# Scores of an attention kernel in two matmuls of 288 columns, and first-pass scores of batch 0 on 128 rows

## The chip, the cores and the metric

The kernel runs on one core of one Trainium2 chip. The metric is the device time of one execution in microseconds (us), lower is better: the median of three runs of the kernel before is 1108.2 us (1106.79 to 1108.76).

## What is computed

Attention over 4 batches, 8 heads, 576 positions and a head dimension of 64, with a threshold: of each row of scores only those within tau of the row's maximum are kept. Behind it come two feed-forward layers over the 2304 tokens (512 to 2048 to 512), the first with a hard-swish gate, the second with a sigmoid gate. All in float32.

```python
scores = scale * np.matmul(q, k.transpose(0, 1, 3, 2))
thresh = np.max(scores, axis=-1, keepdims=True) - tau
scores = np.where(scores >= thresh, scores, -1000000000.0)
scores = scores - np.max(scores, axis=-1, keepdims=True)
attn = np.exp(scores)
attn = attn / (np.sum(attn, axis=-1, keepdims=True) + 1e-09)
return np.matmul(attn, v).astype(np.float32)
```

The result, heads side by side, goes through `g = h * clip(h + 3, 0, 6) / 6` between the first pair of weight matrices and through `g = h * sigmoid(1.702 h)` between the second.

## The kernel before, in words

**Units.** `unit` (line 512) handles two heads of one batch, 16 units in all, four for a batch. Its nine query tiles (line 515) are four tiles of 128 queries for each head and one remainder tile, `None`, that holds the last 64 queries of both heads. A tile's scores against all 576 keys go to a buffer `ps` of two PSUM banks, of which there are two (lines 578 and 594). `soft` (line 610) then reduces the row maximum on VectorE (line 620), makes the threshold (line 622 or 624), takes the exponential on ScalarE (line 625) and multiplies it by the mask on VectorE, summing up the row (line 626); after that the `ps` buffer is free.

**Batches 1 to 3** (units 4 to 15, function `full`). To get float32 results from the faster matmul type fp32r, q and k are split into a high and a low part (lines 555 to 562), and the high and low part of q lie on top of one another in the 128 rows. `score2` (line 576) runs k high and then k low, each as a matmul of 512 and one of 64 columns (lines 582 and 583), so four matmuls for a tile and eight for the remainder tile, which takes both heads. In batches 2 and 3 the tiles of e are turned by VectorE and by transfers through DRAM (`blocks`, line 693), in batch 1 by TensorE (`plain`, line 685).

**Batch 0** (units 0 to 3, function `half`, line 788) works in plain fp32: `score` (line 592) multiplies 64 rows of q with 64 rows of k in two matmuls of 288 columns, one head in rows 0 to 63, the other in rows 64 to 127. The first pass takes the first 256 queries of each head, four tiles for a unit, one at a time; the second pass takes the remainder tile on all 128 rows and then the other four tiles in pairs, one of each head together. The queries come in one buffer of 640 columns by four transfers (line 537) and two zero fills (line 535), the keys by two transfers (line 541); VectorE scales the queries by 1/8 (line 547). The first passes of all four units are entered ahead of the second passes, with the first MoE half of batch 0 (`moe_a`, line 836) between.

**Order.** All operations are entered in a `Plan` (line 61) with an engine, a cost in ns and a nominal time, and what they read and write. `settle` (line 220) places them by list scheduling, forward and backward in turn, on the five engines and the DMA, and the program of every engine is emitted in that order. `score2` has a planned cost of 4 or 8 times `pe(SH)`, SH being 288 (line 589). `fill` (line 233) puts matmuls of zeros and ones (line 1134) where the plan leaves TensorE idle. All transfers are issued by SP in the planned order, and each waits in that queue for its buffer. A ring such as `g` (line 807, eight buffers) hands its buffers out in turn.

Of the kernel before, what the change touches and what calls it, by code (L numbers as in the profile page):

```python
# [18 lines left out]
P = 128  # L19
# [242 lines left out]
def tile_top_attention_moe_moe2(  # L262
# [22 lines left out]
    FULL = EXACT = 4  # L285
# [226 lines left out]
    def unit(u, b, j, t0):  # L512

        early, exact = u < FULL, u < EXACT
# [8 lines left out]
        def tile_():  # L523
            return buf("kqv", 12, "st", [P, QC], F32R)

        if exact:
            khb, qhb = tile_(), tile_()
        pieces = [(0, 0, 0, S)] + ([(1, 0, 0, 256), (1, 256, 320, 256), (1, 576, 256, 64)] if b == 0 else [(1, 0, 64, 512), (1, 576, 0, 64)])

        def of_head(x, hd):  # L530
            return [(x, ("z", hd))] + [(x, (h, o)) for h, o, _, _ in pieces if h == hd]

        def load_q(x, ap):
            for hd, z in ((0, 576), (1, 512)):
                add(POOL, 100, K("ld"), "qz", lambda hd=hd, z=z: nc.gpsimd.memset(ap()[64 * hd:64 * hd + 64, z:z + 64], 0.0), [], [(x, ("z", hd))])
            for hd, o, i, n in pieces:
                move(K("ld"), "ldq", 256 * n, lambda hd=hd, o=o, i=i, n=n: nc.sync.dma_start(out=ap()[64 * hd:64 * hd + 64, o:o + n], in_=q2[b, 2 * j + hd, :64, i:i + n]), [], [(x, (hd, o))])

        def load_k(x, ap):
            for hd in range(2):  # L540
                move(K("ld"), "ldk", 256 * S, lambda hd=hd: nc.sync.dma_start(out=ap()[64 * hd:64 * hd + 64, :S], in_=k2[b, 2 * j + hd, :64]), [], [(x, hd)])

        if exact:
# [32 lines left out]
        def score2(s):  # L576

            ps, t = buf("ps", 2, "ps", [P, 1024]), tiles[s]

            def mm(hd, q0, st, sp):  # L580
                for w, a, z in ((khs, st, False), (kls, False, sp)):
                    for c0, c1 in ((0, 512), (512, S)):
                        nc.tensor.matmul(ps.t[:, c0:c1], qss[hd].t[:, q0:q0 + P], w[hd].t[:, c0:c1], start=a, stop=z)  # L583

            def run():
                for hd in range(2) if t is None else t[:1]:
                    mm(hd, t[1] * P + 128 * hd if t else 0 if hd else 512, t is not None or hd == 0, t is not None or hd == 1)

            add(PE, (4 if t else 8) * pe(SH), K("S", s), "S", run, [x[hd] for hd in (range(2) if t is None else t[:1]) for x in (qss, khs, kls)], [ps])
            soft(s, ps, lambda: ps.t[:, :S], lambda e: e.t)  # L590

        def score(ss):

            pss = {s: buf("ps", 2, "ps", [P, 1024]) for s in ss}

            def two(s, n=512):
                return pss[s].t.rearrange("p (j s) -> p j s", j=2)[:, :, :n]

            def mm():
                for i in range(2):  # L600
                    for s in ss:
                        t = tiles[s]
                        rows, q0 = (slice(0, P), 512) if t is None else (slice(64 * t[0], 64 * t[0] + 64), t[1] * P)
                        nc.tensor.matmul(two(s)[:, i, :SH], f32(qhb.t)[rows, q0:q0 + P], f32(khb.t)[rows, i * SH:(i + 1) * SH], start=True, stop=True)  # L604

            add(PE, 4 * 243 + 300 + 40 * (len(ss) > 1), K("S", ss[0]), "S", mm, [qhb, khb] if len(ss) > 1 or tiles[ss[0]] is None else of_head(qhb, tiles[ss[0]][0]) + [(khb, tiles[ss[0]][0])], [pss[s] for s in ss])
            for s in ss:
                soft(s, pss[s], lambda s=s: two(s, SH), lambda e: e.t.rearrange("p (j s) -> p j s", j=2))

        def soft(s, ps, scores, like):  # L610
# [6 lines left out]
            def ev():  # L617
                return like(e)

            add(DVE, 665, K("R", s), "R", lambda: nc.vector.tensor_reduce(out=nm.t[:, c], in_=scores(), op=ALU.max, axis=AX.XY if len(scores().shape) == 3 else AX.X, negate=True), [ps], [(nm, s)])  # L620
# [4 lines left out]
            add(ACT, 624, K("X", s), "X", lambda: nc.scalar.activation(out=ev(), in_=scores(), func=ACTF.Exp, bias=nm.t[:, c]), [ps, (nm, s)], [e])  # L625
            add(DVE, 729, K("M", s), "M", lambda: nc.vector.scalar_tensor_tensor(out=ev(), in0=scores(), scalar=th.t[:, c], in1=ev(), op0=ALU.is_ge, op1=ALU.mult, accum_out=sm.t[:, c]),  # L626
# [566 lines left out]
```

## Time and profile before

| | us |
|---|---|
| median of three runs | 1108.2 |
| lowest and highest | 1106.79, 1108.76 |
| the profiled execution | 1111.02 |
| its span, first to last instruction | 1108.9 |

The span is what the profile's shares refer to. PE is TensorE's matmuls, PEld its weight loads, DVE VectorE, ACT ScalarE, POOL GpSimd, SP the engine that issues the transfers. Times of rows in order of time count from the start of the span. The end of a matmul in the trace is modelled and runs past the start of the next, so the price of a matmul is read from one start to the next. The granted clock is TensorE's, as a share of full speed (2.4 GHz); it has two levels, 1.0 and 0.5, and a stretch shows their mean. An fp32 matmul stands in the trace as two records, an fp32r matmul as one.

### The profile page before, as it was taken

To read this page: it belongs to the slowest core of one execution; us is meant where nothing else is said; L and a number is where in the kernel's file an instruction comes from. 1 tells how busy PE (TensorE), PEld (TensorE's weight loads), DVE (VectorE), ACT (ScalarE), POOL (GpSimd) and SP (SyncE) were. 2 spreads that over 40 slices of the span, in tenths; PEclk is the share of its full clock that TensorE was granted. 3 is DMA by queue.
4 is the path that set the end of the run, shared out by engine and by line. 5 is a ranking of instruction groups with operands and counts; after the bars stand their busy time and mean duration, and the time that the engine had idled before them with its cause. 6 is when DMAs were issued, how large, how long until landed. Compare 5 with 4: busy or idle time off the path is not lost.

```text
span 1108.9 us, 20750 instructions
## 1 busy us (share of the span) xinstructions
PE 1076.6 (97%) x7672; PEld 973.6 (88%) x7672; DVE 729.0 (66%) x1482; ACT 639.3 (58%) x1340; POOL 510.2 (46%) x590
## 2 busy tenths in 40 slices
PE   8999999999899999999999999999999999999998
PEld 6677788977788889899999999989998889889888
DVE  6788866667687776267877432778787674653634
ACT  4698767665575655466555323566656665443533
POOL 1578867765686755356466223551313322001100
PEclk8899999998999999999999999999999999999999
DMA  6234322256878686635664312335545443312202
GB/s 201 91 116 132 101 82 59 91 147 191 221 234 247 182 253 186 182 107 157 203 204 128 91 54 65 124 103 169 180 145 175 151 136 115 114 39 77 91 1 72
DMA packets 89733, 150.19 MB, mean 135 GB/s; under 512 B 8864, under 2 KB 50976, under 8 KB 87584
## 3 DMA queue, kind: packets, MB, share of 16 engines
q1 hardware_dynamic: 89632, 148.87, 44.1%
q8 instruction: 60, 0.98, 0.4%
q14 instruction: 41, 0.34, 0.1%
HBM read 101.52 MB, written 47.32 MB: 134 GB/s over the span
## 4 chain that ended last, share of the span: by engine, by line
PE 77%; DVE 8%; DMA 7%; ACT 4%; issue 2%; POOL 2%; SPq 0%; DVEq 0%; POOLq 0%; ACTq 0%
PE py L834 24%; PE pm L814 16%; PE pm L971 13%; PE pm L834 7%; PE ps L583 5%; PE pm L755 5%; PE pm L677 3%; PE ps L604 2%; DMA qk<-in_k_dram 1%; DVE e L626 1%; DVE nm L620 1%; DVE outlring L369 1%; PE pm L736 1%; DVE tc L369 1%; ACT e L625 1%
## 5 line engine op out<-in xcount | busy, mean ns | idle before, releaser
L834 PE MATMUL py<-g,outhring 128*128 128x512 f32 (+2 forms) x1152 | 288.1, 337 | 2.0 <-DVE g L369 1.4
L834 PEld LDWEIGHTS py<-g,outhring 128*128 128x128 f32 x1152 | 193.7, 188 | 20.7 <-DVE g L369 4.0
L834 PE MATMUL py<-g,outlring 128*128 128x512 f32 (+2 forms) x576 | 193.4, 336 | 0.0
L814 PE MATMUL pm<-xh,inhring 128*128 128x256 f32 (+1 forms) x512 | 155.6, 304 | 0.2
L814 PE MATMUL pm<-xl,inhring 128*128 128x256 f32 (+1 forms) x512 | 150.8, 295 | 0.0
L814 PE MATMUL pm<-xh,inlring 128*128 128x256 f32 (+1 forms) x512 | 150.8, 294 | 0.0
L971 PE MATMUL pm<-outhring,inhring 128*128 128x256 f32 x512 | 144.5, 282 | 3.4 <-ACT u L366 1.9
L971 PE MATMUL pm<-outlring,inhring 128*128 128x256 f32 x512 | 143.7, 281 | 0.0
L971 PE MATMUL pm<-outhring,inlring 128*128 128x256 f32 x512 | 143.5, 280 | 0.0
L620 DVE TENSOR_REDUCE nm<-ps 128x1 f32<-128x576 f32 x144 | 106.5, 751 | 44.5 <-PE ps L583 37.5
L626 DVE SCALAR_TENSOR_TENSOR e<-ps,th,e 128x576 f32<-128x576 f32 x128 | 102.6, 811 | 35.6 <-ACT e L625 34.8
L369 POOL TENSOR_TENSOR g<-t,g 128x256 fp32r<-128x256 f32 (+1 forms) x104 | 87.2, 842 | 82.1 <-ACT g L366 76.3
L826 DVE SCALAR_TENSOR_TENSOR t<-t,pm 128x256 f32<-128x256 f32 (+1 forms) x128 | 57.1, 448 | 95.3 <-ACT t L825 94.9
L834 PEld LDWEIGHTS py<-g,outlring 128*128 128x128 f32 x576 | 108.2, 188 | 10.0
L834 PE MATMUL pm<-g,outhring 128*128 128x256 f32 (+1 forms) x512 | 109.9, 307 | 0.0
L369 POOL TENSOR_TENSOR wmstg<-wmstg,wrstg 128x512 uint32<-128x512 uint32 x48 | 64.6, 1346 | 94.9 <-DVE wmstg L422 75.3
L369 POOL TENSOR_TENSOR g<-tc,g 128x512 fp32r<-128x512 f32 x24 | 31.9, 1328 | 165.1 <-ACT g L366 160.3
L825 ACT ACTIVATE t<-pm,half 128x256 f32<-128x256 f32 (+1 forms) x128 | 63.5, 498 | 72.7 <-PE pm L814 66.5
L971 PEld LDWEIGHTS pm<-outhring,inhring 128*128 128x128 f32 x512 | 96.8, 189 | 7.3 <-ACT u L366 2.3
L583 PE MATMUL ps<-kqv 128*128 128x512 f32 x480 | 93.6, 326 | 9.3 <-DVE e L626 9.1
L625 ACT ACTIVATE e<-ps,nm 128x576 f32<-128x576 f32 x128 | 93.1, 733 | 16.5 <-DVE nm L620 14.8
L971 PEld LDWEIGHTS pm<-outlring,inhring 128*128 128x128 f32 x512 | 96.9, 189 | 2.5
(110 smaller groups left out, 2452.0 us busy)
## 6 DMA issues: line engine op xcount, KB each, us to landing
turned<-tr SPq DMA_DIRECT2D x16, 1024.0 KB, 4.6
et<-turned SPq DMA_DIRECT2D x64, 256.0 KB, 5.9
wrawstg<-in_w1i_dram SPq DMA_DIRECT2D x16, 512.0 KB, 3.8
wrawstg<-in_w1o_dram SPq DMA_DIRECT2D x16, 512.0 KB, 3.7
wrawstg<-in_w2i_dram SPq DMA_DIRECT2D x16, 512.0 KB, 3.7
wrawstg<-in_w2o_dram SPq DMA_DIRECT2D x16, 512.0 KB, 4.0
qk<-in_k_dram SPq DMA_DIRECT2D x24, 288.0 KB, 4.2
qk<-in_q_dram SPq DMA_DIRECT2D x24, 288.0 KB, 4.2
```

Of the source, the lines that this page charges most:

```text
L369: return lambda: (nc.vector if eng == DVE else nc.gpsimd).tensor_tensor(out=o(), in0=a(), in1=b(), op=op)
L583: nc.tensor.matmul(ps.t[:, c0:c1], qss[hd].t[:, q0:q0 + P], w[hd].t[:, c0:c1], start=a, stop=z)
L620: add(DVE, 665, K("R", s), "R", lambda: nc.vector.tensor_reduce(out=nm.t[:, c], in_=scores(), op=ALU.max, axis=AX.XY if len(scores().shape ...
L625: add(ACT, 624, K("X", s), "X", lambda: nc.scalar.activation(out=ev(), in_=scores(), func=ACTF.Exp, bias=nm.t[:, c]), [ps, (nm, s)], [e])
L626: add(DVE, 729, K("M", s), "M", lambda: nc.vector.scalar_tensor_tensor(out=ev(), in0=scores(), scalar=th.t[:, c], in1=ev(), op0=ALU.is_ge, ...
L677: nc.tensor.transpose(pt.t[:kn, o:o + P], e_of[s].t[:, keys(k)], id_b.t)
L755: nc.tensor.matmul(o.t[64 * hd:64 * hd + 64, c:c + n], v_(k, hd), x(p, k, hd), start=k == 0, stop=k == 4)
L814: nc.tensor.matmul(ph.t[:, :n], a, v, start=(cc == 0 and i == 0), stop=(cc == KC - 1 and i == 2))
L825: add(ACT, 93 + act(n), K("RL"), "RL", lambda: nc.scalar.activation(out=tt_(), in_=pt(), func=ACTF.Relu, scale=1.0 / 6.0, bias=half_b.t), ...
L826: add(DVE, dve(n), K("GT"), "GT", lambda: nc.vector.scalar_tensor_tensor(out=tt_(), in0=tt_(), scalar=1.0, in1=pt(), op0=ALU.min, op1=ALU. ...
L834: nc.tensor.matmul(py.t[:, :n], a, v, start=(st and i == 0), stop=(sp and i == 2))
L971: nc.tensor.matmul(o.t[:, :n], u.t[:, ws], v.t[:, xv], start=(st and kk == 0 and i == 0), stop=(sp and kk == 1 and i == 2), skip_group_che ...
```

## The change

Three things change.

1. `score2` splits the 576 keys in the middle: two matmuls of 288 columns for each part of k in place of 512 and 64, one in each of the two PSUM banks. `soft` reads all score buffers as two runs of 288 columns.
2. In batch 0's first pass, `score1` takes 128 rows: the queries of one head stand in a buffer of their own, `qzb`, with zeros in the other head's 64 rows, and are multiplied with the keys of both heads. It waits for both keys. Its planned cost is 4 x 243 ns without the 300 ns that `score` adds.
3. The queries of batch 0 are loaded in two lots: 256 columns of each head for the first pass, with zero fills of 64 x 256, and 384 columns of both for the second pass in three transfers, with a nominal time 4 us later. Each lot is scaled by one instruction over 128 rows, 512 and 384 columns wide; before, unit 0 scaled its heads apart. `qzb` is taken from ring `g`.

```diff
-        if exact:
-            load_q(qhb, lambda: f32(qhb.t))
-            load_k(khb, lambda: f32(khb.t))
-            for rows, hds in ((slice(0, 64), (0,)), (slice(64, P), (1,))) if u == 0 else ((slice(0, P), (0, 1)),):
-                add(DVE, 69 + 0.521 * QC, K("qs"), "qs", lambda rows=rows: nc.vector.tensor_scalar(out=f32(qhb.t)[rows], in0=f32(qhb.t)[rows], scalar1=sc_b.t[rows], scalar2=1.0, op0=ALU.mult, op1=ALU.mult),
-                    [sc_b], [x for hd in hds for x in of_head(qhb, hd)])
+        if early:
+            khb, qhb, qzb = tile_(), tile_(), buf("g", HF, "gp", [P, 640], F32R)
+            for hd in range(2):
+                r, o = slice(64 * hd, 64 * hd + 64), slice(64 - 64 * hd, P - 64 * hd)
+                add(POOL, 260, K("ld"), "qz", lambda o=o, c=256 * hd: nc.gpsimd.memset(f32(qzb.t)[o, c:c + 256], 0.0), [], [(qzb, ("z", hd))])
+                add(POOL, 100, K("ld"), "qz", lambda o=o, c=256 + 64 * hd: nc.gpsimd.memset(f32(qhb.t)[o, c:c + 64], 0.0), [], [(qhb, ("z", hd))])
+                move(K("ld"), "ldq", 256 * 256, lambda r=r, c=256 * hd, h=2 * j + hd: nc.sync.dma_start(out=f32(qzb.t)[r, c:c + 256], in_=q2[b, h, :64, :256]), [], [(qzb, (hd, 0))])
+                move(K("ld"), "ldk", 256 * S, lambda r=r, h=2 * j + hd: nc.sync.dma_start(out=f32(khb.t)[r, :S], in_=k2[b, h, :64]), [], [(khb, hd)])
+            add(DVE, 69 + 0.521 * 512, K("qs"), "qs", lambda: nc.vector.tensor_scalar(out=f32(qzb.t)[:, :512], in0=f32(qzb.t)[:, :512], scalar1=sc_b.t, scalar2=1.0, op0=ALU.mult, op1=ALU.mult),
+                [sc_b], [(qzb, x) for hd in range(2) for x in (("z", hd), (hd, 0))])
+            for hd, o, i, n in ((0, 0, 256, 320), (1, 320, 256, 64), (1, 0, 320, 256)):
+                move(K("ld") + 4000, "ldq", 256 * n, lambda hd=hd, o=o, i=i, n=n: nc.sync.dma_start(out=f32(qhb.t)[64 * hd:64 * hd + 64, o:o + n], in_=q2[b, 2 * j + hd, :64, i:i + n]), [], [(qhb, (hd, o))])
+            add(DVE, 69 + 0.521 * 384, K("qs") + 4000, "qs", lambda: nc.vector.tensor_scalar(out=f32(qhb.t)[:, :384], in0=f32(qhb.t)[:, :384], scalar1=sc_b.t, scalar2=1.0, op0=ALU.mult, op1=ALU.mult), [sc_b], [qhb])
...
         def score2(s):
-            ps, t = buf("ps", 2, "ps", [P, 1024]), tiles[s]
+            ps, t = buf("ps", 2, "ps", [P, 2, 512]), tiles[s]
             def mm(hd, q0, st, sp):
                 for w, a, z in ((khs, st, False), (kls, False, sp)):
-                    for c0, c1 in ((0, 512), (512, S)):
-                        nc.tensor.matmul(ps.t[:, c0:c1], qss[hd].t[:, q0:q0 + P], w[hd].t[:, c0:c1], start=a, stop=z)
+                    for i in range(2):
+                        nc.tensor.matmul(ps.t[:, i, :SH], qss[hd].t[:, q0:q0 + P], w[hd].t[:, i * SH:(i + 1) * SH], start=a, stop=z)
...
+        def score1(s):
+            ps, (hd, m) = buf("ps", 2, "ps", [P, 2, 512]), tiles[s]
+            q0 = 256 * hd + m * P
+            def mm():
+                for i in range(2):
+                    nc.tensor.matmul(ps.t[:, i, :SH], f32(qzb.t)[:, q0:q0 + P], f32(khb.t)[:, i * SH:(i + 1) * SH], start=True, stop=True)
+            add(PE, 4 * 243, K("S", s), "S", mm, [(qzb, x) for x in (("z", hd), (hd, 0))] + [khb], [ps])
+            soft(s, ps)
...
         def score(ss):
+            if len(ss) == 1 and tiles[ss[0]] is not None:
+                return score1(ss[0])
...
```

## Rows read from the trace of the kernel before

**Rows 1.** The page: busy time, share of the span and count, by engine.

```profile
PE 1076.6 (97%) x7672; PEld 973.6 (88%) x7672; DVE 729.0 (66%) x1482; ACT 639.3 (58%) x1340; POOL 510.2 (46%) x590
```

**Rows 2.** The chain of waits over the whole span, by line.

```profile
by line: PE py L834 23.7%; PE pm L814 15.8%; PE pm L971 13.3%; PE pm L834 6.7%; PE ps L583 5.4%; PE pm L755 4.9%; PE pm L677 3.1%; issue 2.2%; PE ps L604 1.8%; DMA qk<-in_k_dram 1.4%; DVE e L626 1.3%; DVE nm L620 1.1%; DVE outlring L369 1.1
```

**Rows 3.** The chain within 113 to 240 and within 240 to 400, by line.

```profile
by line: PE ps L583 24.1%; PE pm L755 16.0%; PE pm L814 15.7%; PE pm L834 15.3%; PE pm L677 14.0%; DVE nm L620 2.8%; PE pm L736 2.3%; ACT et L680 2.1%; issue 1.7%; ACT e L625 1.6%; DVE e L626 1.4%; PE pm L1134 1.0%; DVE er L626 0.7%; DVE wm
...
by line: PE ps L583 13.1%; PE pm L755 12.0%; PE pm L834 11.0%; DMA qk<-in_k_dram 10.0%; PE pm L814 9.2%; DMA et<-turned 5.3%; issue 4.3%; DMA qk<-in_q_dram 4.0%; DMA turned<-tr 3.6%; POOL kqv L369 3.5%; DVE e L626 3.4%; POOL e L639 3.2%; DV
```

**Rows 4.** Windows: length, busy by engine, granted clock, DMA share, GB/s.

```profile
113.00:240.00 127.00, 123.02 (x963) 107.20 (x962) 86.11 (x208) 88.31 (x180) 93.33 (x127) 1.00 0.29 89
240.00:400.00 160.00, 147.82 (x1141) 131.07 (x1140) 115.23 (x248) 96.27 (x229) 110.05 (x155) 0.98 0.76 219
```

**Rows 5.** TensorE in order of time: start, length, line, tiles, form, count.

```profile
281.34 2.13 PE L583 MATMUL ps<-kqv 128*128 128x512 f32 x12
...
283.54 0.30 PE L814 MATMUL pm<-xl,inhring 128*128 128x320 f32 x1
...
284.12 0.31 PE L814 MATMUL pm<-xh,inlring 128*128 128x320 f32 x1
```

**Rows 6.** The same view: twelve 256-column matmuls (L834) up to the next line.

```profile
131.96 0.40 PE L834 MATMUL pm<-g,outhring 128*128 128x256 f32 x2
...
133.39 0.30 PE L677 MATMUL pm<-id,e 128*128 128x128 f32 x1
```

**Rows 7.** Groups on VectorE in 0 to 50: count, busy us, mean ns.

```profile
L626 DVE SCALAR_TENSOR_TENSOR e<-ps,th,e 128x576 f32<-128x576 f32 x14 | 11.4, 814 | 4.8 <-ACT e L625 4.7
```

**Rows 8.** The same view in 113 to 431.

```profile
L626 DVE SCALAR_TENSOR_TENSOR e<-ps,th,e 128x576 f32<-128x576 f32 x94 | 75.5, 810 | 28.4 <-ACT e L625 27.7
```

**Rows 9.** TensorE in order of time: a first-pass tile on 64 rows, alone.

```profile
20.01 1.24 PE L604 MATMUL ps<-kqv 64*128 64x288 f32 x4
21.17 1.09 PE L677 MATMUL pm<-id,e 128*128 128x128 f32 x8
```

**Rows 10.** The same view: a remainder tile of batch 0 on 128 rows.

```profile
66.64 1.22 PE L604 MATMUL ps<-kqv 128*128 128x288 f32 x4
67.70 0.38 PE L677 MATMUL pm<-id,e 128*128 128x128 f32 x2
```

**Rows 11.** The same view: two tiles together on 64 rows, second pass.

```profile
70.76 0.28 PE L814 MATMUL pm<-xh,inlring 128*128 128x256 f32 x1
70.97 1.24 PE L604 MATMUL ps<-kqv 64*128 64x288 f32 x8
72.14 0.33 PE L677 MATMUL pm<-id,e 128*128 128x128 f32 x1
```

**Rows 12.** The same view: two first-pass tiles overlapped.

```profile
11.76 3.36 PE L604 MATMUL ps<-kqv 64*128 64x288 f32 x8 [0.72 <-DVE e L626]
```

**Rows 13.** Windows 0 to 20 and 260 to 280, columns as in rows 4.

```profile
0.00:20.00 20.00, 17.57 (x68) 12.93 (x68) 12.30 (x34) 5.96 (x8) 3.49 (x18) 0.83 0.54 147
...
260.00:280.00 20.00, 18.04 (x134) 14.45 (x134) 11.93 (x26) 9.45 (x23) 9.96 (x14) 0.83 0.64 184
```

**Rows 14.** SP's issues in order of time: start, length, line, transfer, count.

```profile
1.76 0.59 SPq L541 DMA_DIRECT2D kqv<-in_k_dram  x1
2.39 1.87 SPq L537 DMA_DIRECT2D kqv<-in_q_dram  x3
...
15.68 0.59 SPq L409 DMA_DIRECT2D wrawstg<-in_w1i_dram  x1
```

**Rows 15.** Transfers issued in 0 to 18: count, KB each, us to landing.

```profile
kqv<-in_k_dram SPq DMA_DIRECT2D x8, 144.0 KB, 2.9
```

**Rows 16.** TensorE in order of time: the first score.

```profile
5.10 1.25 PE L604 MATMUL ps<-kqv 64*128 64x288 f32 x4
```

**Rows 17.** Groups on VectorE in 0 to 20: scaling the queries.

```profile
L547 DVE TENSOR_SCALAR kqv<-kqv,sc 128x640 f32<-128x640 f32 (+1 forms) x5 | 2.7, 548 | 2.8 <-DMA kqv<-in_q_dram 2.8
```

**Rows 18.** Groups on GpSimd in 0 to 20: zero fills of the queries.

```profile
L535 POOL MEMSET kqv<- 64x64 f32 x8 | 1.2, 145 | 0.6 <-POOLq L1181 0.3
```

More of the change, by code (lines that the diff above doesn't have):

```diff
@@ L284, in tile_top_attention_moe_moe2 @@
     CH = [(0, 256), (256, 320)]
-    FULL = EXACT = 4
+    FULL = 4
     scale = 0.125
@@ L512, in unit @@
     def unit(u, b, j, t0):
-        early, exact = u < FULL, u < EXACT
+        early = u < FULL
         tiles = [(0, 0), (1, 0), (0, 1), (1, 1), None, (0, 2), (1, 2), (0, 3), (1, 3)]
@@ L524, in tile_ @@
             return buf("kqv", 12, "st", [P, QC], F32R)
-        if exact:
[L527 to L537, printed above, removed]
@@ L589, in score2 @@
             add(PE, (4 if t else 8) * pe(SH), K("S", s), "S", run, [x[hd] for hd in (range(2) if t is None else t[:1]) for x in (qss, khs, kls)], [ps])
-            soft(s, ps, lambda: ps.t[:, :S], lambda e: e.t)
+            soft(s, ps)
[6 more added lines that the diff above has]
+            add(PE, 4 * 243, K("S", s), "S", mm, [(qzb, x) for x in (("z", hd), (hd, 0))] + [khb], [ps])
+            soft(s, ps)
         def score(ss):
-            pss = {s: buf("ps", 2, "ps", [P, 1024]) for s in ss}
-            def two(s, n=512):
-                return pss[s].t.rearrange("p (j s) -> p j s", j=2)[:, :, :n]
+            if len(ss) == 1 and tiles[ss[0]] is not None:
+                return score1(ss[0])
+            pss = {s: buf("ps", 2, "ps", [P, 2, 512]) for s in ss}
             def mm():
@@ L602, in mm, with soft @@
                         t = tiles[s]
-                        rows, q0 = (slice(0, P), 512) if t is None else (slice(64 * t[0], 64 * t[0] + 64), t[1] * P)
-                        nc.tensor.matmul(two(s)[:, i, :SH], f32(qhb.t)[rows, q0:q0 + P], f32(khb.t)[rows, i * SH:(i + 1) * SH], start=True, stop=True)
-            add(PE, 4 * 243 + 300 + 40 * (len(ss) > 1), K("S", ss[0]), "S", mm, [qhb, khb] if len(ss) > 1 or tiles[ss[0]] is None else of_head(qhb, tiles[ss[0]][0]) + [(khb, tiles[ss[0]][0])], [pss[s] for s in ss])
+                        rows, q0 = (slice(0, P), 256) if t is None else (slice(64 * t[0], 64 * t[0] + 64), t[1] * P - 256)
+                        nc.tensor.matmul(pss[s].t[:, i, :SH], f32(qhb.t)[rows, q0:q0 + P], f32(khb.t)[rows, i * SH:(i + 1) * SH], start=True, stop=True)
+            add(PE, 4 * 243 + 300 + 40 * (len(ss) > 1), K("S", ss[0]), "S", mm, [qhb, khb], [pss[s] for s in ss])
             for s in ss:
-                soft(s, pss[s], lambda s=s: two(s, SH), lambda e: e.t.rearrange("p (j s) -> p j s", j=2))
-        def soft(s, ps, scores, like):
+                soft(s, pss[s])
+        def soft(s, ps):
             t = tiles[s]
@@ L617, in ev @@
             def ev():
-                return like(e)
-            add(DVE, 665, K("R", s), "R", lambda: nc.vector.tensor_reduce(out=nm.t[:, c], in_=scores(), op=ALU.max, axis=AX.XY if len(scores().shape) == 3 else AX.X, negate=True), [ps], [(nm, s)])
+                return e.t.rearrange("p (j s) -> p j s", j=2)
+            add(DVE, 665, K("R", s), "R", lambda: nc.vector.tensor_reduce(out=nm.t[:, c], in_=ps.t[:, :, :SH], op=ALU.max, axis=AX.XY, negate=True), [ps], [(nm, s)])
             if b in TURNED:
@@ L624, in soft @@
                 add(DVE, 121, K("TH", s), "TH", lambda: nc.vector.tensor_scalar(out=th.t[:, c], in0=nm.t[:, c], scalar1=-1.0, scalar2=nt_b.t, op0=ALU.mult, op1=ALU.add), [(nm, s), nt_b], [(th, s)])
-            add(ACT, 624, K("X", s), "X", lambda: nc.scalar.activation(out=ev(), in_=scores(), func=ACTF.Exp, bias=nm.t[:, c]), [ps, (nm, s)], [e])
-            add(DVE, 729, K("M", s), "M", lambda: nc.vector.scalar_tensor_tensor(out=ev(), in0=scores(), scalar=th.t[:, c], in1=ev(), op0=ALU.is_ge, op1=ALU.mult, accum_out=sm.t[:, c]),
+            add(ACT, 624, K("X", s), "X", lambda: nc.scalar.activation(out=ev(), in_=ps.t[:, :, :SH], func=ACTF.Exp, bias=nm.t[:, c]), [ps, (nm, s)], [e])
+            add(DVE, 729, K("M", s), "M", lambda: nc.vector.scalar_tensor_tensor(out=ev(), in0=ps.t[:, :, :SH], scalar=th.t[:, c], in1=ev(), op0=ALU.is_ge, op1=ALU.mult, accum_out=sm.t[:, c]),
                 [ps, (th, s)], [e, (sm, s)])
```

3 lines of the change are left out of this document (removed).

## The prediction, made before the changed kernel was run

> **What bounds the kernel now.** I read the share of busy time first, then the chain of work that ended last, stage by stage, and then TensorE's rows in order of time. TensorE is busy for 97% of the span and no other engine passes 66% [rows 1]. The chain spends 5.4% of the span in the score line L583 [rows 2]. The scores of batches 1 to 3 lie between 113 and 431 us. From 113 to 240 the chain is nearly all TensorE, with L583 at 24.1%; from 240 to 400, where the tiles of e are turned by DMA, L583 has 13.1%, and transfers of k, q and of turned tiles have 10.0 + 5.3 + 4.0 + 3.6 = 22.9% [rows 3]. In that second stretch TensorE is idle for 160.00 - 147.82 = 12.2 us and the DMA engines are 0.76 busy, against 0.29 before 240 [rows 4]. So a cheaper score should shorten the first stretch one for one and the second only in part.
>
> **Batches 1 to 3: the price of a tile now.** A tile of 128 queries is four matmuls, 512 + 64 columns twice. Twelve of them, three tiles, begin at 281.34; the second matmul of the next line begins at 283.54, and that line's regular step is 0.146 us (283.54 to 284.12 in four). Three tiles therefore occupy 283.54 - 281.34 - 0.146 = 2.05 us, 0.684 us each [rows 5]. A pair costs 0.342 us for 576 columns, as much as 750 columns would at 0.146 us for 320: the narrow matmul costs several times its columns.
>
> **The price after.** No row shows four 288-column matmuls of this type (batch 0's are plain fp32, each in two records). The nearest rows are 320 columns at 0.146 us [rows 5] and 256 columns at 1.43 us for twelve (131.96 to 133.39), 0.119 us each [rows 6], both with a weight load for each matmul, as here. 288 lies half way: 0.1325 us, with the bounds 0.119 and 0.146. A tile is then 0.530 us (0.476 to 0.584) and saves 0.154 us (0.100 to 0.208). There are 12 units with 8 such tiles and one remainder tile of eight matmuls: 10 tile prices each, 120 in all. Taken off TensorE: 120 x 0.154 = **18.5 us** (12.0 to 25.0).
>
> **What of it lies on the path.** L583's part of the chain is 5.4% of 1108.9 = 59.9 us, out of its own 120 x 0.684 = 82.1 us. In 240 to 400 it is 13.1% of 160 = 21.0 us; the other 38.9 us keep the saving whole: 38.9/82.1 x 18.5 = 8.8 us. In 240 to 400 the share is 21.0/82.1 x 18.5 = 4.7 us; TensorE arrives earlier there, but k and q stand in SP's queue with the transfers of turned tiles [rows 3], so a transfer is late next. I keep half, 2.4 us (bounds 0 and 4.7). Scores together: **-11.2 us**. Their readers now take two runs of 288 columns instead of one of 576, as batch 0's already do: its masked product takes 814 ns [rows 7], that of the later batches 810 [rows 8]. If these 4 ns count in each of VectorE's two readings and ScalarE's one, 108 tiles make 108 x 12 ns = 1.3 us, beside TensorE's work; I take 0.
>
> **Batch 0, first pass.** Sixteen tiles run on 64 rows now. A tile that runs alone lasts from 20.01 to 21.17, 1.16 us [rows 9]; the remainder tile, on 128 rows already, from 66.64 to 67.70, 1.06 us [rows 10]. Entering costs too: the 256-column matmul ahead of a 64-row score takes 0.21 us (70.76 to 70.97) [rows 11], where such a matmul has 0.119 [rows 6]. So 0.19 us less for each of the 12 tiles that run alone: -2.3 us. The other four run as two overlapped groups of eight records; the one at 11.76 lasts 3.36 us [rows 12], in a stretch whose granted clock is 0.83, part of it at the lower level of 1.2 GHz [rows 13]. On 128 rows its two tiles follow one another, 2 x 2 x 1.06 = 4.24 us at half clock: +0.9 us for each group, less if the clock is up, so +1.8 to 0 for both. Together -0.5 us, between -2.3 and 0.
>
> **Loads, zeros, scaling.** For its first score unit 0 now needs the first q and the first k transfer (the k issued at 1.76); afterwards it needs both heads of both, since one 128-row instruction scales the padded queries and the matmul reads all rows of k. SP issues one in about 0.63 us (1.76, 2.39), so the fourth leaves at 3.03 [rows 14]; k takes 2.9 us to land [rows 15], so 5.9 us, against a first score at 5.10 [rows 16]: up to +1.0 us at the start. The second score comes sooner, as k of head 1 now waits behind the three q pieces (2.39, 1.87 us). SP issues 7 transfers for a unit in place of 6, 4 x 0.63 = 2.5 us more of its queue, but only 16 instead of 24 stand ahead of the last first-pass score, so weights (first issued at 15.68 [rows 14]) may leave up to 8 x 0.63 = 5.0 us earlier; and a late q piece can hold up the second pass. The planner decides which. VectorE scales 512 + 384 columns for 640, which took 548 ns [rows 17]: 0.77 us for a unit, 3.1 in all for 2.7, while the first pass has 1.0 us less of it. GpSimd gets eight wider zero fills beside eight of the old size: 64 x 64 took 145 ns [rows 18], so four times that, 0.58 us, bounds each, 4.6 us in all, on an engine busy for 3.49 of the first 20 us [rows 13]; a late fill of unit 0 would hold the first score. The padded queries borrow four buffers of ring g, whose next user, the MoE of batch 0, comes after the first pass: nothing, unless that pass runs late. All of this I put at -0.8 us, nearer to nothing than to either end, as it rests on the order: between -5.0 (weights earlier, all of it on the path) and +3 (first score and order both worse). Batch 0 together: **-1.3 us**.
>
> **The sum.** -11.2 - 1.3 = -12.5 us. The profiled execution took 1111.0 us (its span of 1108.9 and 2.1 around it), so 1098.5 in its terms; it is 2.8 us over the median of the runs, 1108.2, so **1095.7 us** in theirs. The times below are in those.
>
> **Rivals.**
> (a) The saving is swallowed: nothing remains in 240 to 400, and elsewhere the chain moves to VectorE, which waits for scores but is not idle enough to take all of them earlier. With half of the 8.8 us left and batch 0 at zero: 1108.2 - 4.4 = 1103.8. For it: DMA 0.76 busy. Against it: from 113 to 240 VectorE works 86.11 of 127 us, GpSimd 93.33 [rows 4]. Chance 0.19.
> (b) The pair's extra cost is a fixed one for each pair and not the narrow matmul's, so 288 + 288 still costs 0.342 us: the change does not do what it says. Only batch 0 is left, 1106.9. Against it: 256 and 320 columns, each with its weight load, show no such step. Chance 0.04.
> (c) Slower: TensorE, sooner done, waits longer for transfers in 240 to 400, and its clock falls to the lower level, 1.2 GHz of 2.4. The clock of 0.83 in 260 to 280 [rows 13] is 20 x 0.17/0.5 = 6.8 us at that level, 3.4 us lost. From the fourth further such spell on (12.5/3.4 = 3.7) the change loses; with five, 1095.7 + 17 = 1112.7. For it: 12.2 us of idle time are there already. Against it: only one spell came of them. Chance 0.07. The Trainium skill, TensorE: Matmul & The Clock Gate, section "HAM oscillation — how this bites in real kernels", says that a TensorE which idles between groups of matmuls falls back to the low clock and starts the next group there; by that rule denser waiting is a loss, and the trace agrees with it in that one spell.
> (d) Half-height tiles are worth half a full one, and 128 rows give that away. Two together took 1.17 us (70.97 to 72.14) [rows 11], 0.585 each against 1.06: 16 x 0.48 = +7.6 us in place of -1.3, so 1108.2 - 11.2 + 7.6 = 1104.6. Against it: twelve of the sixteen run alone, at 1.16. Chance 0.02. The Trainium skill, TensorEngine Tiling, section "Theoretical Speedup", gives up to twice the rate where the contraction is 64; the trace has it where two tiles run together, and not for a single one.
>
> **How the numbers follow.** The forecast has 0.68; its own range, from the bounds of the score's price, of the kept share and of batch 0 (not all at their ends at once), is 1087 to 1101. Taking in (a) carries the upper end to 1104; the lower end of 1086 leaves room for the low-clock spell to vanish. A measurement of this kernel tells about 0.2%, 2.2 us, from no change. Faster: 0.68 + 0.19 + 0.02, less 0.01 for the weak end of (a): 0.88. The same: (b) and that end, 0.05. Slower: (c), 0.07.
>
> **What would show it.** Right: 288-column matmuls with 0.53 us from tile to tile; the scores' share of the chain down to about 4%; the score region ending some 11 us sooner, with the MoE stages behind it as long as before; first-pass tiles of 1.06 us, with no longer step ahead of them. Wrong: TensorE's idle time in 240 to 400 grown by as much as the tiles shrank (a), a pair still at 0.34 us (b), more stretches at 0.83 (c), a first pass that ends later than now.

## The result and the profile after

| | before | after |
|---|---|---|
| median, us | 1107.7 (4 runs, 1106.79 to 1108.76) | 1095.58 (4 runs, 1093.03 to 1100.24) |
| ratio, 95% interval | | 0.9896 (0.9866 to 0.9926) |
| profiled execution, its span | 1111.02, 1108.9 | 1093.03, 1091.2 |

The change takes 12.1 us off; 12.5 were forecast. The spans of the two profiled executions lie 17.7 us apart, more than the medians, since the execution of before took longer than its timed runs and that of after is the shortest of its four. What is read from one profile against the other is therefore checked below against medians. In the new file the score line L583 is L573, the first-pass scores are L589, the second-pass ones L605, and most other lines move on by one.

The page's busy times, in the same columns as [rows 1]:

```profile
PE 1058.7 (97%) x7706; PEld 970.0 (89%) x7706; DVE 724.2 (66%) x1485; ACT 638.1 (58%) x1340; POOL 515.3 (47%) x598
```

TensorE still fills 97% of a shorter span, and its busy time went down by 1076.6 - 1058.7 = 17.9 us. So its shares look as before, and only the chain tells what moved. The chain over the whole span, by line, answers to [rows 2]:

```profile
by line: PE py L835 23.4%; PE pm L815 14.1%; PE pm L972 13.8%; PE pm L835 6.2%; PE pm L756 4.1%; PE ps L573 3.6%; issue 2.9%; PE pm L678 2.0%; DMA qk<-in_k_dram 2.0%; DVE e L627 1.6%; DMA qk<-in_q_dram 1.3%; ACT e L626 1.3%; DVE nm L621 1.3
```

Then the chain in the two stretches that correspond to [rows 3], now 109 to 230 and 230 to 390 us, and the windows for [rows 4] and the start (columns as there):

```profile
by line: PE ps L573 17.5%; PE pm L756 16.7%; PE pm L835 11.3%; PE pm L678 10.3%; PE pm L815 8.2%; ACT e L626 4.5%; issue 4.4%; DVE e L627 3.7%; ACT et L681 3.5%; POOL kqv L369 2.6%; DVE nm L621 2.5%; POOL e L640 2.4%; PE pm L737 2.3%; ACT k
...
by line: DMA qk<-in_k_dram 13.4%; DMA qk<-in_q_dram 8.6%; PE pm L815 8.2%; PE ps L573 7.4%; PE pm L835 5.8%; PE pm L756 5.7%; issue 5.1%; POOL e L640 5.0%; DVE e L627 4.9%; POOL kqv L369 4.5%; DVE tr L699 4.0%; DMA turned<-tr 3.8%; DVE nm L
...
0.00:20.00 20.00, 16.30 (x85) 13.77 (x86) 12.38 (x36) 8.06 (x12) 6.36 (x26) 1.00 0.64 188
109.00:230.00 121.00, 116.11 (x949) 103.26 (x950) 83.26 (x209) 85.93 (x177) 89.76 (x125) 1.00 0.28 90
230.00:390.00 160.00, 146.58 (x1172) 134.11 (x1172) 118.25 (x252) 99.00 (x234) 111.78 (x156) 0.97 0.78 222
```

The scores went from 5.4% to 3.6% of the chain. In the first stretch other engines have come up beside TensorE: ScalarE's exponential has 4.5% (1.6% before), the masked product 3.7% (1.4%). In the second, k and q alone are 22.0%, where they were 14.0%: a transfer is late next, as the forecast had it.

TensorE in order of time: twelve new score matmuls between 256-column ones (count last, as in [rows 5]), then, in the first pass of batch 0, the first score and a later tile.

```profile
243.04 1.76 PE L573 MATMUL ps<-kqv 128*128 128x288 f32 x12
244.63 0.28 PE L815 MATMUL pm<-xh,inhring 128*128 128x256 f32 x1
244.75 0.28 PE L815 MATMUL pm<-xl,inhring 128*128 128x256 f32 x1
244.87 0.28 PE L815 MATMUL pm<-xh,inlring 128*128 128x256 f32 x1
...
6.04 2.62 PE L589 MATMUL ps<-kqv,g 128*128 128x288 f32 x8
...
14.84 1.21 PE L589 MATMUL ps<-kqv,g 128*128 128x288 f32 x4
15.88 1.04 PE L678 MATMUL pm<-id,e 128*128 128x128 f32 x8
```

Three tiles take 244.75 - 243.04 - 0.12 = 1.59 us, 0.530 each; over 41 places read in this way the median is 0.532 us, and 0.686 over 43 places of before. A first-pass tile lasts 15.88 - 14.84 = 1.04 us. The first score begins at 6.04, 0.94 us after that of before [rows 16].

SP's issues, GpSimd's zero fills and VectorE's groups at the start, and the masked product in 109 to 417 (columns as in [rows 14], [rows 7]):

```profile
1.16 1.18 SPq L532 DMA_DIRECT2D g<-in_q_dram  x2
2.38 1.24 SPq L533 DMA_DIRECT2D kqv<-in_k_dram  x2
...
11.84 0.59 SPq L409 DMA_DIRECT2D wrawstg<-in_w1i_dram  x1
...
0.71 2.77 POOL L530 MEMSET g<- 64x256 f32 x8 [0.29 <-POOLq L1182]
...
L534 DVE TENSOR_SCALAR g<-g,sc 128x512 f32<-128x512 f32 x4 | 2.0, 490 | 3.0 <-DMA g<-in_q_dram 3.0
...
L538 DVE TENSOR_SCALAR kqv<-kqv,sc 128x384 f32<-128x384 f32 x1 | 0.4, 420 | 0.8 <-DMA kqv<-in_q_dram 0.8
...
L627 DVE SCALAR_TENSOR_TENSOR e<-ps,th,e 128x576 f32<-128x576 f32 x95 | 76.5, 810 | 30.4 <-ACT e L626 29.2
```

The first weights leave SP at 11.84 instead of 15.68; a fill takes 2.77/8 = 0.35 us; a unit's scaling takes 0.490 + 0.420 = 0.91 us; reading two runs of 288 columns costs VectorE nothing (810 ns, as in [rows 8]).

**A ruler through the program.** VectorE makes 144 row-maximum reductions, one for each query tile, and their starts can be counted off in the trace of any of these kernels. The table gives the start of some of them in us; the 37th is the first of batch 1, the 144th the last of batch 3. Below the first line stands the difference to before, in one profiled execution each; the last line compares two experiments with one another.

| | 37th | 79th | 133rd | 144th |
|---|---|---|---|---|
| before | 113.9 | 236.3 | 401.6 | 431.1 |
| after | -4.1 | -10.5 | -12.4 | -13.8 |
| after, second profile | -4.3 | -9.8 | -12.3 | -13.7 |
| split alone | -2.0 | -6.3 | -2.6 | -3.8 |
| split alone, second profile | -3.7 | -7.9 | -9.7 | -11.1 |
| 320 + 256 columns | -1.8 | -5.7 | -6.6 | -7.7 |
| batch 0 alone | -3.3 | -5.3 | -8.2 | -7.9 |
| split less no split, both without turned transfers | -1.3 | -6.1 | -12.9 | -14.4 |

The 113.9 us of before is itself late. Four other profiles with the old batch 0 in the old order (split alone twice, 320 + 256, and 448 + 128 further below) have their 37th reduction at 110.3 to 112.1, against 109.7 to 110.6 with the new batch 0 (after twice, and batch 0 alone). So 2 to 3 us of each difference belong to that one profile, and what is gained from one column to the next says more than the column itself.

From the start of the last score matmul to the first matmul of the second MoE pass the time is as before (282.0 us, 282.5 before); from there to the end it is 392.5 us, 395.5 before.

### The profile page after: what moved, and what is told of

Same layout as the page of the kernel before. It is cut to its first block, busy times and chain, and to the rows that moved or that the text cites. A ratio compares the mean times of both kernels' runs of the same rounds, so it can differ in the third digit from the quotient of the medians.

```text
span 1091.2 us, 20840 instructions
## 1 busy us (share of the span) xinstructions
PE 1058.7 (97%) x7706; PEld 970.0 (89%) x7706; DVE 724.2 (66%) x1485; ACT 638.1 (58%) x1340; POOL 515.3 (47%) x598
## 4 chain that ended last, share of the span: by engine, by line
PE 69%; DVE 9%; DMA 7%; ACT 5%; POOL 4%; issue 3%; SPq 2%; POOLq 0%; DVEq 0%; ACTq 0%
PE py L835 23%; PE pm L815 14%; PE pm L972 14%; PE pm L835 6%; PE pm L756 4%; PE ps L573 4%; PE pm L678 2%; DMA qk<-in_k_dram 2%; DVE e L627 2%; DMA qk<-in_q_dram 1%; ACT e L626 1%; DVE nm L621 1%; DMA wrawstg<-in_w1i_dram 1%; POOL e L640 1%; POOL kqv L369 1%
## 5 line engine op out<-in xcount | busy, mean ns | idle before, releaser
L835 PE MATMUL pm<-g,outhring 128*128 128x256 f32 (+1 forms) x512 | 107.7, 301 | 0.5 <-POOL g L369 0.4
L626 ACT ACTIVATE e<-ps,nm 128x576 f32<-128x576 f32 x128 | 93.0, 733 | 15.2 <-DVE nm L621 13.4
L815 PEld LDWEIGHTS pm<-xh,inhring 128*128 128x128 f32 x512 | 98.0, 191 | 4.2 <-DVE t L827 2.9
```

The lines of the kernel that those rows point to most:

```text
L815: nc.tensor.matmul(ph.t[:, :n], a, v, start=(cc == 0 and i == 0), stop=(cc == KC - 1 and i == 2))
L835: nc.tensor.matmul(py.t[:, :n], a, v, start=(st and i == 0), stop=(sp and i == 2))
```

## The experiments

### The changed kernel once more

> The changed kernel itself, once more, on one chip with the runs beside it. If the two parts simply add (split alone 0.9952, batch 0 alone 0.9988 of the kernel before): 0.994, some 6.6 us less. Rival, they help each other, because in the new order of the instructions less of the cheaper tile is lost: 0.990, 10 to 13 us less, as measured first.

Measured: 1096.63 us (7 runs) against 1106.42 (21 runs), ratio 0.9924 (0.9896 to 0.9952), so -8.4 us of 1107. The tile's median is 0.531 us. The direction holds; the size lies between the two expectations.

The first question of the others was how the 12 us divide between the two parts, the second where the rest of the split's 18.5 us stays.

### The split alone, in the old order of every engine

```diff
-                    for c0, c1 in ((0, 512), (512, S)):
-                        nc.tensor.matmul(ps.t[:, c0:c1], qss[hd].t[:, q0:q0 + P], w[hd].t[:, c0:c1], start=a, stop=z)
+                    for i in range(2):
+                        nc.tensor.matmul(ps.t[:, 512 * i:512 * i + SH], qss[hd].t[:, q0:q0 + P], w[hd].t[:, i * SH:(i + 1) * SH], start=a, stop=z)
```

> Batches 1 to 3 in two matmuls of 288 columns, batch 0 as before, so every engine keeps the order of the kernel before. My theory: a tile costs 0.53 us in place of 0.684, scores start at 113 us as before and end about 10 us earlier (at 421 in place of 431), and the time is 1107.7 - 11.2 = 1096.5 us (1093 to 1101). Rival, the earlier start of batch 1 and the new order carry most of the gain: the score stretch of 318 us shrinks by 5 us or less and the time stays over 1102.

Measured: 1099.51 us (12 runs) against 1103.89 (30 runs), ratio 0.9952 (0.9929 to 0.9975): -5.3 us, half of the -11.2 expected. The tile costs 0.530 us. As the profiled execution was the longest of the twelve (1105.85), the same kernel was measured once more.

> The first measurement of the split alone gave a ratio of 0.9952 to the kernel before, and its profiled execution was the slowest of twelve (1105.85 us against a median of 1099.51), with a mean clock of 0.94 in 240 to 396. Theory, the transfers: the split keeps its saving up to 240 us and the transfers of 240 to 400 are late next in any execution; a second profile then shows TensorE idle for 15 to 18 us between 240 and 396 (12.2 in 160 us before) at whatever clock, the score region ends 3 to 8 us sooner than before, and the ratio is again near 0.995 (0.993 to 0.997). Rival, the clock: the part that was missing went to the low-clock spells of that one execution; a second profile with fewer of them shows the score region ending 9 to 12 us sooner, with idle time near 12 us, and the ratio is near 0.990.

Measured: 1100.22 us (8 runs) against 1105.47 (13 runs), ratio 0.9947 (0.9927 to 0.9968): -5.9 us. Windows of 240 to 400 in the first and the second execution, and the chain of the second in 240 to 396:

```profile
240.00:400.00 160.00, 142.31 (x1103) 129.22 (x1104) 112.40 (x238) 93.69 (x223) 103.92 (x145) 0.94 0.73 215
```

```profile
240.00:400.00 160.00, 145.01 (x1172) 130.04 (x1174) 118.52 (x253) 97.61 (x233) 107.46 (x151) 0.98 0.76 220
...
by line: DMA qk<-in_q_dram 19.2%; POOL kqv L369 10.3%; issue 9.9%; POOL e L639 6.6%; DVE e L626 5.0%; DVE tr L698 4.8%; DVE nm L620 3.8%; POOL g L369 3.8%; DMA qk<-in_k_dram 3.6%; DMA turned<-tr 3.5%; PE pm L755 3.2%; PE pm L814 3.1%; SPq L
```

Before, TensorE was idle there for 12.2 us at a clock of 0.98 [rows 4]. Now it is idle for 17.7 us at 0.94 and for 15.0 us at 0.98, and the score line has dropped out of the rows shown of the second chain. Both measurements agree on 5 to 6 us, half of the 11.2 forecast. The two profiles differ in that stretch: from the 79th to the 133rd reduction the first gives back 3.7 us (-6.3 to -2.6), the second keeps 1.8 (-7.9 to -9.7). The second score region ended 11.1 us sooner, as the rival had it, but 3.7 of these lie ahead of the first split matmul; the ratio is that of the transfers' theory.

The second profile also says what part the clock has. Between the 79th and the 133rd reduction the mean clock is 0.979 in it and in the profile of before, which makes 6.8 us at the lower level in each; TensorE is idle for 16.9 us there, 12.3 before. So in this pair the longer waiting takes the saving and the clock has no part in it; the first profile has 20.5 us at the lower level beside 17.9 of waiting. The profile of 320 + 256 columns, a third one at the same price and in the same order, has 17.2 us of idle time in 240 to 400 at 0.97, and keeps 0.9 us from the 79th to the 133rd.

### Without the transfers of turned tiles

If transfers take the rest, a kernel without turned tiles must keep more. It turns all tiles on TensorE (`TURNED = ()`), with and without the split, in one order.

```diff
-    TURNED = (2, 3)
+    TURNED = ()
```

> The kernel before with batches 2 and 3 turned by TensorE, as batch 1 is, so without the transfers of e through DRAM. It is the partner of the next run. Expected: TensorE has 16 transposes more for each unit, 8 units, about 0.11 us each in two records, some 25 us more, so slower by 10 to 25 us than the kernel before; DMA share in the score stretch under 0.5.

> The same without the transfers of e, with the split at 288; every engine's order is that of its partner. Theory, the transfers of turned tiles take the missing part of the saving in batches 2 and 3: here nearly all of 18.5 us comes off, 13 to 18 us less than its partner. Rival, the saving is lost to VectorE, ScalarE and GpSimd, which pace the scores in all batches: again only 4 to 7 us less. Rival, it is lost to the low clock: the gain lies between, and the partner with the split shows more low stretches than the one without.

Measured: 1122.25 us (6 runs), 1.0138 of before (1.0113 to 1.0163), and with the split 1108.49 (12 runs), 1.0014 (0.9997 to 1.0031). The split takes off 13.8 us here. Windows of 240 to 400, without and with the split, and the chain of the first:

```profile
240.00:400.00 160.00, 158.72 (x1294) 145.08 (x1293) 92.25 (x235) 104.70 (x215) 104.79 (x145) 1.00 0.25 72
...
by line: PE pm L814 22.9%; PE pm L834 22.5%; PE ps L583 20.7%; PE pm L755 15.8%; PE pm L677 15.8%; PE pm L1134 0.8%; ACT et L680 0.8%; issue 0.5%; ACT kqv L366 0.4%; ACT e L625 0.0%; ACT xr L366 0.0%
```

```profile
240.00:400.00 160.00, 158.18 (x1336) 148.15 (x1334) 94.60 (x243) 106.90 (x220) 108.07 (x149) 1.00 0.24 71
```

TensorE is the whole chain, its clock stays at 1.00, the DMA engines are busy for a quarter of the time instead of three quarters, and the same edit is worth 2.5 times as much. From the 79th reduction to the 133rd it gains 6.8 us (last line of the table), against +3.7 and -1.8 with the transfers. So the split's saving is real TensorE time, and what swallows it in 240 to 400 comes with the way in which tiles are turned: shown. That it is the transfers themselves is not shown by this pair, which also takes the transposes off VectorE (busy for 115.23 us before, 92.25 here) and gives TensorE more to do. For the transfers speak the chains: k and q have 22.0% in the changed kernel, and 19.2 + 3.6 = 22.8% in the second profile of the split alone, against 14.0% before.

### Batch 0 alone

The changed kernel in its own order, with 512 + 64 columns and readers of one run of 576 put back in batches 1 to 3.

```diff
-                    for i in range(2):
-                        nc.tensor.matmul(ps.t[:, i, :SH], qss[hd].t[:, q0:q0 + P], w[hd].t[:, i * SH:(i + 1) * SH], start=a, stop=z)
+                    for c0, c1 in ((0, 512), (512, S)):
+                        nc.tensor.matmul(ps.t.rearrange("p j s -> p (j s)")[:, c0:c1], qss[hd].t[:, q0:q0 + P], w[hd].t[:, c0:c1], start=a, stop=z)
```

> The changed batch 0, batches 1 to 3 with 512 + 64 columns as before; every engine has the order of the changed kernel. My theory: batch 1's scores start at 109 us in place of 113, the score stretch is about 318 us long again, and the time is 1 to 4 us under the kernel before, 1103.7 to 1106.4. Rival, what batch 0 gains is taken back behind it by transfers that are not earlier: within 0.5 us of 1107.7. Rival, the new order alone is worth as much as the cheaper tile: under 1101.

Measured: 1103.47 us (12 runs), 0.9988 (0.997 to 1.0006): -1.3 us, between -3.3 and +0.7. The median of the mean clocks of its runs is 0.997, where the runs of before beside it have 0.994.

### The first pass on 64 rows, and without early filler

Two parts of the new batch 0 undone in the changed kernel. The first multiplies only the 64 rows of a tile's own head, with the new buffers, loads and order. The second drops the matmuls of zeros and ones that the plan puts into TensorE's gaps ahead of a planned 50 us.

```diff
-                    nc.tensor.matmul(ps.t[:, i, :SH], f32(qzb.t)[:, q0:q0 + P], f32(khb.t)[:, i * SH:(i + 1) * SH], start=True, stop=True)
+                    nc.tensor.matmul(ps.t[:, i, :SH], f32(qzb.t)[64 * hd:64 * hd + 64, q0:q0 + P], f32(khb.t)[64 * hd:64 * hd + 64, i * SH:(i + 1) * SH], start=True, stop=True)
```

> The changed kernel, with the first pass of batch 0 multiplied on the 64 rows of its head as before, from the same buffers, after the same waits and in the same order. My theory: 0.1 us more for each of the 16 tiles that runs alone and 0.09 ahead of it, so 1 to 3 us more than the changed kernel, 1096.5 to 1098.5, and scores of batch 1 that start 1 to 3 us later. Rival, VectorE and the loads pace the first pass: no difference, 1095.6. Rival, two tiles on 64 rows share the array: earlier, under 1094.

Measured: 1099.49 us (12 runs), 0.9957 (0.9938 to 0.9976). TensorE in order of time, the tile that answers to the one of 14.84 above:

```profile
14.62 1.24 PE L589 MATMUL ps<-kqv,g 64*128 64x288 f32 x4
15.78 1.09 PE L678 MATMUL pm<-id,e 128*128 128x128 f32 x8
```

A lone tile takes 1.16 us again. Half-height tiles are not the faster way here. Whether the kernel is slower by them than the changed one cannot be told: the intervals 0.9938 to 0.9976 and 0.9896 to 0.9952 overlap.

```diff
-                if count > 0:
+                if count > 0 and s >= 50000:
```

> The changed kernel without the matmuls of zeros and ones that fill TensorE's idle time in the first 50 us of the plan; all other instructions in the same order. My theory, that part of batch 0's gain is the clock: the granted clock falls again to 0.93 or less in some stretches of the first 60 us, batch 1's scores start 2 to 4 us later than 109, and the time is 1097.5 to 1099.5. Rival, the clock is held up by the 128-row scores themselves: it is low only until about 10 us and the time stays within 1 us of the changed kernel's 1095.6.

Measured: 1097.78 us (7 runs), 0.9937 (0.9913 to 0.9961). The window of 0 to 20:

```profile
0.00:20.00 20.00, 10.40 (x25) 6.82 (x26) 10.26 (x29) 5.36 (x7) 5.65 (x24) 0.82 0.63 191
```

The clock of the start is back at 0.82; TensorE had been busy for half of these 20 us, where with the filler it is busy for 16.30 at 1.00. The 37th reduction comes 2.2 us later than in the changed kernel (112.0 against 109.8), but the 144th does not (416.8 against 417.3). The filler's gain at the start did not reach the end in this pair of profiles; the medians leave it open.

### What a narrow matmul costs

Two other cuts of the 576 columns in the old order, to tell a cost of the pair from one of the narrow matmul.

```diff
-                    for c0, c1 in ((0, 512), (512, S)):
-                        nc.tensor.matmul(ps.t[:, c0:c1], qss[hd].t[:, q0:q0 + P], w[hd].t[:, c0:c1], start=a, stop=z)
+                    for c0, c1 in ((0, 320), (320, S)):
+                        nc.tensor.matmul(ps.t[:, 192 + c0:192 + c1], qss[hd].t[:, q0:q0 + P], w[hd].t[:, c0:c1], start=a, stop=z)
```

> Batches 1 to 3 in matmuls of 320 + 256 columns, lying side by side across the border of two banks, so that the readers take one run of 576 as before; batch 0 and every engine's order as before. My theory, only the narrow matmul is dear: a tile costs 2 x (0.146 + 0.119) = 0.53 us and the time is that of the split at 288 alone, 0.995 of the kernel before. Rival, the equal halves or the two runs of 288 matter: a tile or its readers differ by over 0.05 us, and the time by 3 us.

Measured: 1101.92 us (9 runs), 0.9945 (0.9923 to 0.9966), as the split in the middle; the tile's median is 0.533 us. The other cut has 448 and 128 columns (`(0, 448), (448, S)` at an offset of 64).

> Batches 1 to 3 in matmuls of 448 + 128 columns; order and batch 0 of the kernel before. It prices the narrow matmul at another width. If a matmul of few columns has a fixed least price of about 0.115 us (what 64 columns cost beside 0.227 for 512), a pair costs 0.20 + 0.115 = 0.315 us and a tile 0.63. Rival, a narrow matmul costs four times its columns (64 columns as 256): 128 columns cost as 512, 0.227, a pair 0.43 and a tile 0.85 us, slower than the kernel before.

Measured: one run of 1098.86 us beside a median of 1105.11 of before; the tile's median is 0.629 us. TensorE in order of time, 320 + 256 and then 448 + 128:

```profile
274.46 1.76 PE L583 MATMUL ps<-kqv 128*128 128x320 f32 x12
276.06 0.31 PE L814 MATMUL pm<-xh,inhring 128*128 128x320 f32 x1
276.21 0.31 PE L814 MATMUL pm<-xl,inhring 128*128 128x320 f32 x1
```

```profile
275.80 1.99 PE L583 MATMUL ps<-kqv 128*128 128x448 f32 x12
277.63 0.36 PE L814 MATMUL pm<-xh,inhring 128*128 128x320 f32 x1
277.83 0.31 PE L814 MATMUL pm<-xl,inhring 128*128 128x320 f32 x1
```

The times go with the widths: 0.119 us for 256 columns and 0.146 for 320 [rows 5, 6] are 0.42 ns a column and 0.011 us besides, so 448 columns are estimated at 0.200 and 512 at 0.227. The pair of 448 + 128 took 0.629/2 = 0.315 us, which leaves 0.115 for 128 columns; 512 + 64 took 0.343, which leaves 0.116 for 64. The narrow matmul, with its own weight load, costs about 0.115 us whether it has 64 columns or 128. The two estimates hold in the traces: from one 512-column matmul of L834 to the next the median is 0.227 us, and a 448-column one at the head of a group (a run of score matmuls) takes 0.200 to 0.202 up to the next.

The traces also show where the price arises. Among the score line's weight loads no two begin less than 0.108 us apart. The next wide matmul begins only 0.03 us after a narrow one of 64 columns (0.06 after one of 128), but then lasts longer: 474 ns (median) behind a narrow one, 396 at the head of a group. In the mean, before (busy us, mean ns):

```profile
L834 PE MATMUL py<-g,outhring 128*128 128x512 f32 x512 | 161.0, 394 | 1.4 <-DVE g L369 1.4
...
L583 PE MATMUL ps<-kqv 128*128 128x512 f32 x240 | 90.8, 460 | 9.3 <-DVE e L626 9.1 <-DVE er L626 0.2
```

The weight load of that wide one begins with the narrow matmul, which is too short to cover it, so the wide one waits; 288 columns, at 0.132 us, cover it, and those matmuls have 298 ns at the head of a group and 294 behind another.

### Two attempts to free the second stretch

Since k and q stand in SP's queue with the turned tiles, ScalarE was made to issue the loads of k and q of batches 1 to 3; the order of TensorE and VectorE is that of the changed kernel.

```diff
-                move(K("ld", 4 * hd), "ldk", 4 * P * S, lambda hd=hd, kr=kr: nc.sync.dma_start(out=kr.t, in_=k2[b, 2 * j + hd]), [], [kr])
-                move(K("ld", 4 * hd), "ldq", 4 * P * S, lambda hd=hd, qr=qr: nc.sync.dma_start(out=qr.t, in_=q2[b, 2 * j + hd]), [], [qr])
+                move(K("ld", 4 * hd), "ldk", 4 * P * S, lambda hd=hd, kr=kr: nc.scalar.dma_start(out=kr.t, in_=k2[b, 2 * j + hd]), [], [kr])
+                move(K("ld", 4 * hd), "ldq", 4 * P * S, lambda hd=hd, qr=qr: nc.scalar.dma_start(out=qr.t, in_=q2[b, 2 * j + hd]), [], [qr])
```

> The changed kernel with the loads of k and q of batches 1 to 3 issued by ScalarE instead of SP, at the same place of the plan; all else in the same order. Theory, k and q are late in batches 2 and 3 because they stand in SP's queue behind issues that wait for the turned tiles to land (30 us of such waits): the score stretch shrinks by 3 to 6 us and the time goes to 0.987 to 0.989 of the kernel before, against 0.9924 for the changed kernel. Rival, the transfers share the DMA engines and are slow themselves (8 to 9 us in place of 4): no gain, 0.991 to 0.994. Rival, ScalarE now waits for free buffers and delays exponentials: slower than the changed kernel, over 0.995.

Measured: 1108.72 us (12 runs), 1.0026 (1.0006 to 1.0047), the whole gain gone, as the second rival had it in size. Windows of 230 to 390, then SP's longest wait in 225 to 390 of the changed kernel (waited for, us in total, times, longest):

```profile
230.00:390.00 160.00, 143.08 (x1157) 130.34 (x1155) 114.00 (x244) 97.70 (x232) 109.44 (x153) 0.98 0.76 222
```

```profile
SPq L704 <- DMA turned<-tr: 30.4, 9, 5.3
```

TensorE is idle for 16.9 us instead of 13.4. SP does spend 30.4 us behind turned tiles, but ScalarE's queue is no better place for the loads: there they stand between its exponentials and copies and leave only after them (that this is what costs the time is argued, not shown). In the chain of 230 to 390 k and q have 28.7% now, 22.0% in the changed kernel. The queue is not all of their lateness, as the first rival said: from issue to landing a load of k takes a median of 6.0 us there and one of q 6.6 in the changed kernel, 5.6 and 7.2 with ScalarE as the issuer, against 2.7 and 2.8 in 113 to 240 before. A fourth buffer for k and q (`buf("qk", 4, ...)` for `buf("qk", 3, ...)`) was the other attempt.

> The changed kernel with four buffers for raw k and q in place of three; the planner makes another order of it from the start. Theory of the waiting queue: a free buffer more lets k and q be issued ahead of the turned tiles, so 2 to 5 us less than the changed kernel, 0.988 to 0.991 of the kernel before. Rival, buffers are not what they wait for: 0.992, with what a new order is worth to either side, 3 us or so.

Measured: 1107.57 us (12 runs), 1.0022 (1.0006 to 1.0039). The plan came out in a new order. In its profile batch 1 already runs late, the 79th reduction at 242.4 against 225.8, and TensorE's granted clock over 109 to 240 is 0.95, where the changed kernel has 1.00; that execution was the longest of the twelve (1113.44 us). So this run says nothing on the buffer alone; it says that another order of nearly the same work can go with a time some 11 us longer.

## Why the prediction was right, and which step of it was not

**Price of a tile: right.** 0.530 us forecast from 256 and 320 columns, 0.532 measured. So 120 x 0.154 = 18.5 us of matmul price left TensorE. That its busy time is 17.9 us less is no second proof: batch 0, the filler and the clock have a part in it, and the two profiles of the split alone have 7.5 and 16.2 us less. Rival (b), a fixed cost of the pair, falls: both cuts into two wide matmuls cost the same (0.530, 0.533), and the extra goes with the narrow one.

**What of it lies on the path: too much by about half.** This is the step that failed: "the other 38.9 us keep the saving whole", with half kept in 240 to 400, -11.2 us together. The split alone is worth -5.3 and -5.9. By stages: 24.1% of 127 us, 30.6 us of L583's chain, lie in 113 to 240, so 30.6/82.1 x 18.5 = 6.9 us of the saving were counted there; the profiles have 4.3 and 4.2 (37th to 79th reduction). For 240 to 400, 2.4 were counted; the profiles have 3.7 lost and 1.8 kept, 6.8 kept without the transfers. Behind it 1.9 were counted and 1.2 to 1.4 came. The share of the chain was an upper bound here: when TensorE gets faster, the exponential and the masked product step into the chain, as the chain of 109 to 230 shows. Rival (a), which said so at 1103.8 us (-4.4), comes nearest for the split alone, though it named VectorE alone.

**Batch 0: the sum right.** -1.3 us forecast and -1.3 measured, though the interval of 4 us around it is wide and holds zero. Of its terms, the tile on 128 rows is 1.04 us (1.06 forecast), the first score 0.94 us later (up to 1.0), the first weights 3.8 us earlier (up to 5.0), a wide fill 0.35 us (bound 0.58), the scaling 0.91 us a unit (0.77). The start of the changed kernel's profiles runs at full clock, 1.00 in place of 0.83 [rows 13], but that is not shown to be the change: with the old batch 0 in the old order three other profiles have 1.00 in 0 to 20 (split alone, 320 + 256, 448 + 128) and one has 0.83 (split alone, second).

**The total: right, though not by its terms, and in part by luck.** The forecast of -12.5 is a ratio of 0.9887, inside the first interval but just outside the second one (0.9896 to 0.9952), which rests on more runs. The larger term was forecast at twice what it measured alone, and nothing that was measured alone makes up for it. The parts measured alone, -5.3 to -5.9 and -1.3, add up to about -7; the whole measured -12.1 and -8.4. A ratio of 0.9937 for -7 lies inside the second interval (0.9896 to 0.9952) and outside the first (0.9866 to 0.9926), and the parts have intervals of their own, so that the whole is worth more than its parts is not shown. In the score stretch of the profiles the parts do add up: from the 37th to the 144th reduction after gains 9.7 us and batch 0's order without the split 4.6, so the split 5.1 in that order too, each from one profile. What remains may be the last 392.5 us (392.9 in the second profile of the changed kernel, 394.1 in the one on 64 rows, 394.5 to 395.5 in the split, batch 0 alone and before), where no instruction changed in kind. TensorE is idle there for 6.1 us in both profiles of the changed kernel and for 8.2 before. Why is open; the order is not the reason, as batch 0 alone and the run with k and q on ScalarE share TensorE's order with the changed kernel and have 395.5 and 396.7 us.

**Rivals (c) and (d).** The low clock did not outweigh the gain: 0.97 in 230 to 390 against 0.98 in 240 to 400 before. (c) is at work in part: the first execution of the split alone has 0.94 with 17.7 us of idle time, and the low clock there is 160 x 0.06/0.5 = 19 us long. The rule on idling between groups of matmuls (the Trainium skill, TensorE: Matmul & The Clock Gate, section "HAM oscillation — how this bites in real kernels") agrees with that execution; the second one, at 0.98 with 15.0 us idle, shows that about as much waiting need not bring as much of the low clock (6.8 us there, as before). (d) falls: on 64 rows a lone tile takes 1.16 us, and the kernel is not faster.

**What would show it.** Scores' share of the chain 3.6% (forecast 4%), region end 13.8 us sooner (forecast 11; 2 to 3 us of it belong to the late profile of before), MoE stages as long as before but for the open 3 us.

## What to carry to other kernels

Cut a row of scores into equal halves rather than into a full bank and a rest: a narrow matmul with its own weight load cost as much here as one four times as wide. Take the chain's share of an operation as the most that a cheaper one saves; ask for each stage which engine or transfer is next, and count on less where several are close (here it was half). Where a planner orders the work, measure each part in a fixed order: the run with four buffers, which came out in an order of its own, stood as far above the changed kernel as the change had gained.

## What the runs showed of the hardware that was not expected

A matmul of 64 and one of 128 columns, each with its own weight load of 128 columns, both take about 0.115 us, where 256 columns take 0.119. The time does not pass in the narrow matmul but in the wide one behind it, which waits for its weights (474 ns long in place of 396); two weight loads in a row begin at least 0.108 us apart.

Executions of one kernel differ by some 10 us: 1099.58 to 1109.15 in 30 runs of the kernel before on one chip. A part of it goes with how long the clock stands at 1.2 GHz: over these runs the time falls by about 0.67 us for each 0.001 of mean granted clock (correlation -0.54). One profile of each kernel therefore settles little under 5 us; the split's two profiles ended their scores 7.3 us apart, at medians 0.7 us apart.
